# A third buffer for the multiplier pairs, a constant tile of ones in the prefix sums, and eight plain matmuls ahead of the third group of tiles

## The chip, the cores and the metric

The kernel runs as one program on one core of a Trainium2 chip. The metric is the device time of one execution in microseconds (us); several executions are timed and their median counts. One further execution is recorded by the hardware profiler, and all rows below come from that one. The engines are named as in the profile: PE multiplies matrices, DVE and ACT work on vectors, POOL fills constants and issues some transfers, SP issues most transfers. PEld is the loading of PE's weights, and a letter q behind a name (SPq) is the engine's queue of instructions that only issue or wait.

## The reference

Three layers follow one another, all in float32.

```python
# 1. linear attention with a complex, data-dependent decay; B, H, S, D = 4, 8, 768, 48
mag = np.sqrt(a_re * a_re + a_im * a_im)
scale = np.minimum(mag, 0.999) / (mag + 1e-06)
a_re_n, a_im_n = (a_re * scale, a_im * scale)
for t in range(S):
    new_re = ar * S_re - ai * S_im          # ar, ai: a_re_n, a_im_n at t
    new_im = ar * S_im + ai * S_re
    S_re, S_im = (new_re + k_t outer v_t, new_im)
    y[:, :, t] = einsum('bhd,bhde->bhe', q[:, :, t], S_re)
# 2. top-1 mixture of experts on the 3072 rows of y: 384 -> 1024 -> 384, 8 experts
out[mask] = gate_w[mask, None] * (np.maximum(xe @ w1[e], 0.0) @ w2[e])
# 3. a second layer on all rows
a = x @ w1
b = x @ w2
return ((a * b @ w3) @ w_out)
```

(`k_t outer v_t` stands for the einsum of the keys and values of one time step.)

## The kernel before, in words

The 768 time steps are cut into three groups (NG), and a group into eight pieces (NPC, 24 pieces in all). Two streams of work are interleaved by `drive` (L742).

The first stream, `elementwise` (L804), goes through the pieces on ACT and DVE. For a piece it loads the multipliers a_re and a_im (`load_a`, L786; one load brings the pair of pieces i and i + 1, 768 KB into one buffer of the tag "a"), squares them on ACT and sums the squares (`root`, L821, called three pieces ahead), makes the normed coefficients (`excess`, `norm`; the product at L843 is the last reader of a pair's buffer), forms the running products of the coefficients step by step on DVE (`prefix`, L852: one product at L862 and one sum at L864 for each time step), and scales queries and keys by them (`keys`, L881; the last product is L894). The sums of squares are made on PE for some pieces (L818) and on DVE for the others (L814). The queries and keys of a piece come by `load_qk` (L798, the load at L801, three buffers). The result of a piece is stored to the memory tensor qkd (L899 to L902). `self.stored` is the tile of the last result.

The second stream, `groups` (L1108), does the attention of a group on PE once the eight pieces of that group are made. `ends` (L949) transposes the group's last running product, copies it to the tile T and, ahead of the first and the second group, lets PE do the eight matmuls of `dense` (L961), whose result nobody reads. Then it loads the keys and values of two units (`loads`, L980; kk from qkd at L991, vz at L989), transposes them (L975), and goes through the eight units of the group. `chain` (L1040) carries the state from unit to unit on PE, ACT and DVE (L1060, L1061, L1067, L1074 to L1076); `scores` (L994), `outputs` (L1011) and `route` (L111) fill the time between. Output tiles are routed to experts and scattered to memory by POOL (L162).

When the last piece is done, the pools of the first stream are closed, and the weights w_out and w3 of the third layer are loaded into their memory (L293, tag "fdr") and split into two halves by `halves` (L315) on DVE and ACT. From about 408 us on PE multiplies them (L352 to L354), then the experts run (`moe`, L444), and last the third layer (`moe2`, L540). `route_end` (L231) makes the prefix sums over the experts with `scan` (L176); two other calls of `scan` are in `segments`, in a branch that these inputs do not take.

Tiles are named by tag, and a planner sets the order of each engine's instructions and the buffer of each tile when the program is built: it simulates the engines with times of its own and takes what is ready first. A tile that takes the memory of a closed pool waits for the readers of what lay there. On the chip the order of every engine and queue is then fixed, and each engine works strictly in this order.

Of the kernel before, what the change touches and what calls it, by code (L numbers as in the profile page):

```python
# [9 lines left out]
F32 = mybir.dt.float32  # L10
# [5 lines left out]
ALU = mybir.AluOpType  # L16
# [7 lines left out]
NE = 8  # L24
# [148 lines left out]
    return pr[:, :NE]  # L173


def scan(nc, sp, src, nm):  # L176

    one8 = sp.tile([128, NE], F32, tag="one8", name="one8" + nm)
    nc.vector.memset(one8, 1.0)
    inc = sp.tile([128, NE], F32, tag=nm + "i", name=nm + "i")  # L180
    nc.vector.tensor_tensor_scan(out=inc, data0=one8, data1=src, initial=0.0, op0=ALU.mult, op1=ALU.add)
    ex = sp.tile([128, NE], F32, tag=nm + "e", name=nm + "e")
    nc.vector.tensor_tensor(out=ex, in0=inc, in1=src, op=ALU.subtract)
    return inc, ex


def segments(tc, S, sp):

    nc = tc.nc
    n = sp.tile([128, NE], F32, tag="ntot", name="ntots")  # L190
    nc.vector.tensor_tensor(out=n, in0=totals(tc, S, "s"), in1=S.ebase, op=ALU.subtract)
    _, off = scan(nc, sp, n, "so")
    seg = sp.tile([128, NE], F32, tag="seg", name="seg")
    nc.vector.tensor_scalar(out=seg, in0=n, scalar1=0.0, scalar2=S.bad, op0=ALU.is_gt, op1=ALU.mult)
    for s in range(NP, NT, NP):
        nc.vector.scalar_tensor_tensor(out=seg, in0=n, scalar=float(s), in1=seg, op0=ALU.is_gt, op1=ALU.add)
    cin, cex = scan(nc, sp, seg, "sc")
    nc.vector.tensor_copy(S.nsegi, cin[:, NE - 1 : NE])
    si = sp.tile([128, MAXSEG], I32, tag="si", name="si")
    nc.gpsimd.iota(si, pattern=[[1, MAXSEG]], base=0, channel_multiplier=0)  # L200
    sf = sp.tile([128, MAXSEG, 1], F32, tag="sf", name="sf")
    nc.vector.tensor_copy(sf[:, :, 0], si)
    t78 = lambda nm: sp.tile([128, MAXSEG, NE], F32, tag=nm, name=nm)
    sfb = sf.to_broadcast([128, MAXSEG, NE])
    soh = t78("soh")
    nc.vector.tensor_tensor(out=soh, in0=sfb, in1=bc(cex, MAXSEG, 1), op=ALU.is_ge)
    s2 = t78("s2")
    nc.vector.tensor_tensor(out=s2, in0=sfb, in1=bc(cin, MAXSEG, 1), op=ALU.is_lt)
    nc.vector.tensor_tensor(out=soh, in0=soh, in1=s2, op=ALU.mult)
    st = t78("st")  # L210
    nc.vector.tensor_tensor(out=st, in0=sfb, in1=bc(cex, MAXSEG, 1), op=ALU.subtract)
    skip = sp.tile([128, 1], F32, tag="skip", name="skip")
    nc.vector.tensor_scalar(out=skip, in0=S.bad, scalar1=float(-NP), scalar2=float(NP), op0=ALU.mult, op1=ALU.add)
    nc.vector.tensor_scalar(out=st, in0=st, scalar1=float(NP), scalar2=skip, op0=ALU.mult, op1=ALU.add)
    nl = sp.tile([128, NE], F32, tag="nl", name="nl")
    nc.vector.tensor_scalar(out=nl, in0=n, scalar1=float(-NP), scalar2=0.0, op0=ALU.add, op1=ALU.max)
    nc.vector.tensor_tensor(out=st, in0=st, in1=bc(nl, MAXSEG, 1), op=ALU.min)
    tab = sp.tile([128, 3, MAXSEG], F32, tag="tabf", name="tabf")
    tmp = t78("tmp")
    for r, base in enumerate((S.ebase, off, S.eidx)):  # L220
        if r < 2:
            nc.vector.tensor_tensor(out=tmp, in0=st, in1=bc(base, MAXSEG, 1), op=ALU.add)
            nc.vector.tensor_tensor(out=tmp, in0=tmp, in1=soh, op=ALU.mult)
        else:
            nc.vector.tensor_tensor(out=tmp, in0=soh, in1=bc(base, MAXSEG, 1), op=ALU.mult)
        nc.vector.reduce_sum(out=tab[:, r], in_=tmp, axis=AX.X)
    nc.vector.tensor_copy(S.tab, tab)
# [3 lines left out]
def route_end(tc, S, sp):  # L231

    nc = tc.nc
    n = sp.tile([128, NE], F32, tag="ntot", name="ntote")
    nc.vector.tensor_tensor(out=n, in0=totals(tc, S, "e"), in1=S.ebase, op=ALU.subtract)
    _, off = scan(nc, sp, n, "off")
    nc.vector.tensor_copy(S.offi, off)
    most = sp.tile([128, 1], F32, tag="most", name="most")
    nc.vector.reduce_max(out=most, in_=n, axis=AX.X)
    nc.vector.scalar_tensor_tensor(out=S.rare, in0=most, scalar=float(NP), in1=S.bad, op0=ALU.is_gt, op1=ALU.max)  # L240
    dlt = sp.tile([128, NE], F32, tag="dlt", name="dlt")
    nc.vector.tensor_tensor(out=dlt, in0=off, in1=S.ebase, op=ALU.subtract)
    step = sp.tile([128, NE], F32, tag="step", name="step")
    nc.vector.tensor_copy(step, dlt)
    nc.vector.tensor_tensor(out=step[:, 1:], in0=dlt[:, 1:], in1=dlt[:, : NE - 1], op=ALU.subtract)
    sh = sp.tile([128, NTT, NE], F32, tag="sh", name="sh")
    nc.vector.tensor_tensor(out=sh, in0=S.pos.unsqueeze(2).to_broadcast([128, NTT, NE]), in1=bc(S.ebase, NTT, 1), op=ALU.is_ge)
    nc.vector.tensor_tensor(out=sh, in0=sh, in1=bc(step, NTT, 1), op=ALU.mult)
    pk = sp.tile([128, NTT], F32, tag="pk", name="pk")
    nc.vector.reduce_sum(out=pk, in_=sh, axis=AX.X)  # L250
    nc.vector.tensor_tensor(out=pk, in0=pk, in1=S.pos, op=ALU.add)
    nc.vector.tensor_copy(S.pki, pk)
    ex = sp.tile([128, NTT, NE], F32, tag="ex", name="ex")
    nc.vector.tensor_tensor(out=ex, in0=S.lg, in1=S.mx.to_broadcast([128, NTT, NE]), op=ALU.subtract)
    nc.scalar.activation(out=ex, in_=ex, func=AF.Exp)
    sm = S.cpool.tile([128, NTT], F32, tag="sm", name="sm", bufs=2)
    nc.vector.reduce_sum(out=sm, in_=ex, axis=AX.X)
    nc.vector.tensor_scalar(out=sm, in0=sm, scalar1=1e-9, scalar2=None, op0=ALU.add)
    nc.vector.reciprocal(sm, sm)
    S.sm = sm  # L260
# [364 lines left out]
D = 48  # L625
C = 64
NG = 3
TP = 8
NPC = C // TP
NPIECE = NG * NPC  # L630
# [11 lines left out]
WARM = 8  # L642
# [135 lines left out]
class Attn:  # L778
# [6 lines left out]

    def load_a(self, i):  # L786

        a = self.ep.tile([128, 2, 2, TP * D], F32, tag="a", name=f"a{i}", bufs=2)
        g, p = divmod(i, NPC)
        src = self.S.a[g].rearrange("r l (p e) -> p l r e", e=TP * D)  # L790
        if i:
            self.nc.sync.dma_start(a, src[p : p + 2].rearrange("n l r e -> l r n e"))
        else:
            for n in range(2):
                self.nc.sync.dma_start(a[:, :, n], src[n])
        return [a[:, :, n] for n in range(2)]
# [7 lines left out]
    def elementwise(self, aside, factors):  # L804

        nc, S, ep, e2 = self.nc, self.S, self.ep, self.e2
# [3 lines left out]
        a, sq, pu, y0, cf, P, s2, px, raw = ({} for _ in range(9))  # L810
# [106 lines left out]
        def chain(*gens):  # L917
            for x in gens:
                yield from x

        for i in (0, 2):
            a[i], a[i + 1] = self.load_a(i)
        raw[0] = self.load_qk(0)
        for i in range(AHEAD):
            root(i)
        yield from chain(excess(0), norm(0), excess(1))
        for i in range(NPIECE + 1):
            if i:
                power(i - 1)
                weigh(i - 1)  # L930
            if i % 2 and i + 3 < NPIECE:
                a[i + 3], a[i + 4] = self.load_a(i + 3)
            if i + AHEAD < NPIECE:
                root(i + AHEAD)
            if i + 1 < NPIECE:
                raw[i + 1] = self.load_qk(i + 1)
            ends = [j >= 0 and j % NPC == NPC - 1 for j in (i - 2, i - 1)]
            rest = [keys(i - 2)] if i > 1 and not ends[0] else []
            if i + 1 < NPIECE:
                rest.append(norm(i + 1))  # L940
            if ends[1]:
                rest.append(keys(i - 1))
            if i + 2 < NPIECE:
                rest.append(excess(i + 2))
            yield from mix(*([prefix(i)] if i < NPIECE else []), chain(*rest))
            if i == NPIECE - 1:
                factors()

    def ends(self, g):  # L949
        nc, S = self.nc, self.S  # L950
        pt = self.pp.tile([R2, 4, 128], F32, tag="tr", name=f"trT{g}", bufs=2)
        for r in range(2):
            nc.tensor.transpose(pt[:, r], self.last[g][:, r].rearrange("p r d -> p (r d)"), self.S.ident)
        self.T = self.st.tile([R2, 2, 2, 4, 2 * NH], F32, tag="T", name=f"T{g}")
        for r in range(2):
            nc.scalar.copy(self.T[:, r].rearrange("e q c (k i h) -> e (q c k) i h", k=2, i=2), pt[:, r].rearrange("e (x h i) -> e x i h", h=NH // 2, i=2))
        if g < NG - 1:
            self.dense(self.stored[:, :512], WARM)
        yield 480

    def dense(self, x, n):  # L961
# [450 lines left out]
```

## Time and profile before

| | |
|---|---|
| median of 3 timed runs | 1000.36 us (999.25 to 1002.5) |
| the profiled execution | 1003.89 us; its span from the first to the last instruction 1002.1 us |
| busy in the span | PE 898.0 us (90%), DVE 609.6 us (61%), ACT 488.5 us (49%), POOL 130.3 us (13%) |
| mean granted clock of PE | 0.946 of full speed |
| instructions | 17063 |

Times within the profile count from the start of the span. Busy time is the time in which an engine executes; a share of it over the whole span mixes stages with different limits, so the stages are read one by one below. An idle time stands in square brackets behind an instruction, with the instruction whose end released it.

### The profile page before, as it was taken

To read this page: it belongs to the slowest core of one execution; us is meant where nothing else is said; L and a number is where in the kernel's file an instruction comes from. 1 tells how busy PE (TensorE), PEld (TensorE's weight loads), DVE (VectorE), ACT (ScalarE), POOL (GpSimd) and SP (SyncE) were. 2 spreads that over 40 slices of the span, in tenths; PEclk is the share of its full clock that TensorE was granted. 3 is DMA by queue.
4 is the path that set the end of the run, shared out by engine and by line. 5 is a ranking of instruction groups with operands and counts; after the bars stand their busy time and mean duration, and the time that the engine had idled before them with its cause. 6 is when DMAs were issued, how large, how long until landed. Compare 5 with 4: busy or idle time off the path is not lost. (4 is left out here: it accounts for less than half of the span.)

```text
span 1002.1 us, 17063 instructions
## 1 busy us (share of the span) xinstructions
PE 898.0 (90%) x6402; PEld 764.9 (76%) x6402; DVE 609.6 (61%) x1374; ACT 488.5 (49%) x1089; POOL 130.3 (13%) x197
## 2 busy tenths in 40 slices
PE   3444899868898999999989999998999999999997
PEld 1222468655786788989979999997888888888886
DVE  6899889798798596576489995443232323232222
ACT  6454588774775687444456665443231312121211
POOL 5111000202002102100232201110000000000001
PEclk8666899998897799999999999999999999999999
DMA  5555976429643985553677655640000000000000
GB/s 189 179 179 182 291 251 201 145 95 306 191 144 127 333 265 159 162 175 107 199 205 183 187 133 137 126 85 2 1 9 24 9 24 9 24 5 28 9 24 31
DMA packets 90182, 128.74 MB, mean 128 GB/s; under 512 B 7232, under 2 KB 72688, under 8 KB 90096
## 3 DMA queue, kind: packets, MB, share of 16 engines
q1 hardware_dynamic: 76300, 82.61, 29.1%
q0 software_dynamic: 10688, 40.36, 11.4%
q10 hardware_dynamic: 3108, 4.65, 1.6%
q8 instruction: 51, 0.84, 0.4%
q14 instruction: 35, 0.29, 0.1%
HBM read 92.38 MB, written 35.22 MB: 127 GB/s over the span
## 5 line engine op out<-in xcount | busy, mean ns | idle before, releaser
L608 DVE TENSOR_TENSOR ab<-asb,pb 128x512 f32<-128x512 f32 x48 | 33.0, 687 | 188.2 <-PE pb L354 184.2
L347 ACT CAST h<-w 128x384 fp32r<-128x384 f32 x128 | 65.5, 514 | 96.5 <-PE ph L353 48.9
L348 DVE TENSOR_TENSOR l<-w,h 128x384 fp32r<-128x384 f32 x128 | 70.5, 554 | 63.7 <-ACT h L347 59.0
L603 ACT COPY asb<-pa 128x512 f32<-128x512 f32 x48 | 28.1, 586 | 121.6 <-PE pa L354 117.0
L818 PE MATMUL x<-s,ident 128*128 128x384 f32 x64 | 35.6, 692 | 49.1 <-ACT s L870 49.0
L347 ACT CAST gh<-ab 128x512 fp32r<-128x512 f32 x48 | 29.7, 620 | 94.7 <-DVE ab L608 90.2
L353 PE MATMUL py<-hl,h 128*128 128x432 f32 x192 | 70.1, 365 | 3.9 <-DVE hl L409 3.9
L352 PE MATMUL py<-hh,h 128*128 128x432 f32 x192 | 69.3, 361 | 2.5 <-ACT hh L408 2.5
L352 PE MATMUL ph<-xh,h 128*128 128x432 f32 x192 | 69.6, 363 | 0.0
L354 PE MATMUL ph<-xh,l 128*128 128x432 f32 x192 | 69.4, 361 | 0.0
L353 PE MATMUL ph<-xl,h 128*128 128x432 f32 x192 | 69.3, 361 | 0.0
L354 PE MATMUL py<-hh,l 128*128 128x432 f32 x192 | 69.1, 360 | 0.0
L862 DVE TENSOR_TENSOR pr<-cf,P 128x192 f32<-128x192 f32 x189 | 66.6, 353 | 3.2
L353 PE MATMUL po<-ol,gh 128*128 128x384 f32 x192 | 64.9, 338 | 0.0
L352 PE MATMUL po<-oh,gh 128*128 128x384 f32 x192 | 64.8, 337 | 0.0
L818 PEld LDWEIGHTS x<-s,ident 128*128 128x128 f32 x64 | 15.0, 257 | 64.6 <-ACT s L870 55.6
L354 PE MATMUL po<-oh,gl 128*128 128x384 f32 x192 | 64.1, 338 | 0.0
L572 POOL DMA_INDIRECT out<-ob,mdp x24 | 23.8, 993 | 305.4 <-DVE ob L571 163.7
L975 PE MATMUL tr<-ident,kk 128*96 128x128 f32 x384 | 57.3, 282 | 5.9 <-DMA kk<-qkd 3.5
L976 ACT COPY qkT<-tr 96x512 f32<-96x512 f32 x96 | 53.4, 590 | 15.6 <-PE tr L975 15.1
L352 PE MATMUL pa<-yh,ah 128*128 128x512 f32 x144 | 57.1, 396 | 3.0 <-ACT yh L347 3.0
L353 PE MATMUL pb<-yl,bh 128*128 128x512 f32 x144 | 57.0, 396 | 0.0
(219 smaller groups left out, 2397.7 us busy)
## 6 DMA issues: line engine op xcount, KB each, us to landing
w<-in_w SPq DMA_DIRECT2D x128, 192.0 KB
kk<-qkd SPq DMA_DIRECT2D x24, 768.0 KB
qkd<-qk POOLq DMA_DIRECT2D x21, 768.0 KB, 6.7
qkr<-in_qk SPq DMA_DIRECT2D x24, 384.0 KB
a<-in_a SPq DMA_DIRECT2D x11, 768.0 KB
fdr<-in_w SPq DMA_DIRECT2D x16, 512.0 KB
fdr<-in_v POOLq DMA_DIRECT2D x12, 512.0 KB, 6.3
xs<-zr POOLq DMA_DIRECT2D x8, 648.0 KB, 7.9
```

What stands on the lines that cost most here:

```text
L347: nc.scalar.copy(H, src)
L348: nc.vector.tensor_tensor(out=L, in0=src, in1=H.bitcast(F32), op=ALU.subtract)
L352: nc.tensor.matmul(out, lh, rh, start=first, stop=False)
L353: nc.tensor.matmul(out, lh, rl, start=False, stop=False)
L354: return nc.tensor.matmul(out, ll, rh, start=False, stop=last)
L572: nc.gpsimd.indirect_dma_start(out=S.outv[j], out_offset=bass.IndirectOffsetOnAxis(ap=S.mdp[:, j, 0:1], axis=0), in_=ob, in_offset=None, b ...
L603: nc.scalar.copy(asb, pa)
L608: nc.vector.tensor_tensor(out=ab, in0=asb, in1=pb, op=ALU.mult)
L818: nc.tensor.matmul(p, S.ident, s[r], start=r == 0, stop=r == 1)
L862: v.tensor_tensor(out=pr, in0=twice(cf[i][:, t]), in1=bc(pv, 2, 1), op=ALU.mult)
L975: nc.tensor.transpose(pt[:, h], qk[:, h0 + h, w], self.S.ident)
L976: nc.scalar.copy(qkT[:, w, h0 : h0 + 4], pt)
```

## The change

Three edits. The tag "a" gets three buffers in place of two, one more pair is loaded at the start, and the loads in the loop bring the pair i + 5 in place of i + 3. `scan` reads its ones from a constant tile in place of a tile that it fills itself. The condition in `ends` goes, so that the eight matmuls of `dense` are issued ahead of the third group too.

```diff
-def scan(nc, sp, src, nm):
-
-    one8 = sp.tile([128, NE], F32, tag="one8", name="one8" + nm)
-    nc.vector.memset(one8, 1.0)
+def scan(S, nc, sp, src, nm):
+
     inc = sp.tile([128, NE], F32, tag=nm + "i", name=nm + "i")
-    nc.vector.tensor_tensor_scan(out=inc, data0=one8, data1=src, initial=0.0, op0=ALU.mult, op1=ALU.add)
+    nc.vector.tensor_tensor_scan(out=inc, data0=S.ones[:, :NE], data1=src, initial=0.0, op0=ALU.mult, op1=ALU.add)
...
-        a = self.ep.tile([128, 2, 2, TP * D], F32, tag="a", name=f"a{i}", bufs=2)
+        a = self.ep.tile([128, 2, 2, TP * D], F32, tag="a", name=f"a{i}", bufs=3)
...
         raw[0] = self.load_qk(0)
+        a[4], a[5] = self.load_a(4)
         for i in range(AHEAD):
             root(i)
...
-            if i % 2 and i + 3 < NPIECE:
-                a[i + 3], a[i + 4] = self.load_a(i + 3)
+            if i % 2 and i + 5 < NPIECE:
+                a[i + 5], a[i + 6] = self.load_a(i + 5)
...
-        if g < NG - 1:
-            self.dense(self.stored[:, :512], WARM)
+        self.dense(self.stored[:, :512], WARM)
         yield 480
```

The three callers of `scan` pass S as well. `dense` itself is unchanged:

```python
    def dense(self, x, n):
        w = self.adds.tile([128, 512], F32, tag="ad", name="dense", bufs=2)
        for _ in range(n):
            self.nc.tensor.matmul(w[:, : x.shape[-1]], self.S.ident, x, start=True, stop=True)
```

## Rows read from the trace of the kernel before

**Rows 1.** The windows view: start:end, length, busy us by engine, PEclk, DMA share, GB/s.

```profile
0.00:108.20 108.20, 48.73 (x82) 23.65 (x82) 89.56 (x223) 58.02 (x121) 24.85 (x86) 0.72 0.58 192
108.20:226.40 118.20, 104.06 (x1154) 78.09 (x1154) 102.84 (x258) 89.73 (x235) 9.39 (x13) 0.96 0.59 187
226.40:322.80 96.40, 85.46 (x1105) 68.41 (x1106) 83.01 (x209) 63.16 (x164) 12.75 (x16) 0.89 0.60 195
322.80:332.40 9.60, 8.43 (x69) 6.67 (x67) 4.15 (x19) 2.89 (x8) 0.57 (x1) 0.68 0.81 217
332.40:413.00 80.60, 78.06 (x1129) 67.14 (x1130) 57.64 (x150) 57.27 (x142) 14.06 (x10) 0.97 0.73 232
413.00:692.00 279.00, 270.51 (x1430) 257.17 (x1429) 189.22 (x393) 143.25 (x296) 44.81 (x47) 0.99 0.56 148
```

**Rows 2.** The waits view: waiter, releaser, us in total, times, longest.

```profile
ACT sq L823 <- DMA a<-in_a: 22.3, 10, 4.4
...
SPq L792 <- DVE cf L843: 20.9, 8, 7.2
```

**Rows 3.** DVE in order of time: start, length, line, [idle before it and releaser].

```profile
28.50 0.56 DVE L887 TENSOR_TENSOR s<-x,s 128x384 f32<-128x384 f32 x1 [1.17 <-PE u L818]
...
44.64 0.56 DVE L831 TENSOR_TENSOR sq<-u,sq 128x384 f32<-128x384 f32 x1 [2.66 <-ACT sq L828]
...
66.76 0.56 DVE L831 TENSOR_TENSOR sq<-u,sq 128x384 f32<-128x384 f32 x1 [0.72 <-ACT sq L828]
...
87.72 0.56 DVE L831 TENSOR_TENSOR sq<-u,sq 128x384 f32<-128x384 f32 x1 [0.70 <-ACT sq L828]
...
135.24 0.56 DVE L839 SCALAR_TENSOR_TENSOR sq<-sq,y 128x384 f32<-128x384 f32 x1 [1.68 <-ACT y L837]
...
177.45 0.56 DVE L814 TENSOR_TENSOR sq<-sq 128x384 f32<-128x384 f32 x1 [0.30 <-ACT sq L823]
...
217.83 0.56 DVE L814 TENSOR_TENSOR sq<-sq 128x384 f32<-128x384 f32 x1 [1.25 <-ACT sq L823]
...
255.13 0.56 DVE L814 TENSOR_TENSOR sq<-sq 128x384 f32<-128x384 f32 x1 [4.66 <-ACT sq L823]
```

**Rows 4.** Order of time on SP, ACT and PE around the last pair's load.

```profile
243.72 0.37 SPq L792 DMA_DIRECT2D a<-in_a  x1
...
254.16 0.84 ACT L823 ACTIVATE sq<-a 128x768 f32<-128x768 f32 x1 [4.45 <-DMA a<-in_a]
...
257.25 0.45 PE L1022 MATMUL y<-z,qkT 96*64 96x48 f32 x2 [3.81 <-ACT xo L1026]
```

**Rows 5.** DVE in order of time: idle stretches without a pair's load behind them.

```profile
62.18 0.56 DVE L887 TENSOR_TENSOR s<-x,s 128x384 f32<-128x384 f32 x1 [0.32 <-ACT s L879]
...
197.69 0.69 DVE L1007 TENSOR_TENSOR at<-sc,mask 128x512 f32<-128x512 f32 x1 [4.76 <-PE x L818]
...
249.75 0.56 DVE L814 TENSOR_TENSOR s<-s 128x384 f32<-128x384 f32 x1 [0.97 <-ACT s L870]
```

**Rows 6.** The seam ahead of the third group: DVE, PE, and two windows.

```profile
320.99 1.76 DVE L894 TENSOR_TENSOR qk<-P,qkr 128x1536 f32<-128x1536 f32 x1
...
332.40 1.94 PE L975 MATMUL tr<-ident,kk 128*96 128x128 f32 x8 [0.90 <-DMA kk<-qkd]
...
324.35:332.40 8.05, 6.88 (x34) 5.17 (x32) 2.73 (x17) 2.88 (x7) 0.00 (x0) 0.68 0.90 246
332.40:339.07 6.67, 5.71 (x32) 5.36 (x32) 0.99 (x3) 3.29 (x12) 3.98 (x4) 0.62 1.08 363
```

**Rows 7.** PE in order of time: the plain matmuls at the first two seams.

```profile
108.24 8.83 PE L965 MATMUL dense<-qk,ident 128*128 128x512 f32 x16 [2.34 <-DVE qk L894]
...
226.48 9.68 PE L965 MATMUL dense<-qk,ident 128*128 128x512 f32 x16 [2.18 <-DVE qk L894]
```

**Rows 8.** SP's loads of w_out at the third seam, and the memset's line.

```profile
330.14 4.04 SPq L293 DMA_DIRECT2D fdr<-in_w_out  x5
...
L179 DVE MEMSET one8off<- x1: 65/65/65, 328.2 to 328.2; 128x8 f32 x1
```

More of the change, by code (lines that the diff above doesn't have):

```diff
@@ L191, in segments @@
     nc.vector.tensor_tensor(out=n, in0=totals(tc, S, "s"), in1=S.ebase, op=ALU.subtract)
-    _, off = scan(nc, sp, n, "so")
+    _, off = scan(S, nc, sp, n, "so")
     seg = sp.tile([128, NE], F32, tag="seg", name="seg")
@@ L196, in segments @@
         nc.vector.scalar_tensor_tensor(out=seg, in0=n, scalar=float(s), in1=seg, op0=ALU.is_gt, op1=ALU.add)
-    cin, cex = scan(nc, sp, seg, "sc")
+    cin, cex = scan(S, nc, sp, seg, "sc")
     nc.vector.tensor_copy(S.nsegi, cin[:, NE - 1 : NE])
@@ L235, in route_end @@
     nc.vector.tensor_tensor(out=n, in0=totals(tc, S, "e"), in1=S.ebase, op=ALU.subtract)
-    _, off = scan(nc, sp, n, "off")
+    _, off = scan(S, nc, sp, n, "off")
     nc.vector.tensor_copy(S.offi, off)
```

## The prediction

> **What bounds the kernel now.** I read the stages first, then the waits of ACT and SP, then DVE's order of time with the idle stretch ahead of each instruction, and last PE's order at the seams between the groups. The stage table [rows 1] shows three stretches of the scan (0 to 108.2, 108.2 to 226.4, 226.4 to 322.8 us): each ends when the last piece of a group has been multiplied out and stored, and only then can PE fetch that group's keys. DVE is busy 89.56 of 108.20, 102.84 of 118.20 and 83.01 of 96.40 us there, more than any other engine in the first and about level with PE in the other two. After the seam of 9.6 us PE does one more group (78.06 of 80.60 us) and then has work without a break (270.51 of 279.00 us). So a microsecond taken from the first 323 us moves all that follows; one taken from DVE after it moves nothing.
>
> The loads of the multiplier pairs show in the waits: ACT stood 22.3 us in ten waits for them, and SP stood 20.9 us in eight waits for the product that frees a pair's buffer [rows 2]. The loads are late because they are issued late. ACT's wait counts only where DVE runs dry behind it, and [rows 3] is the list of these: eight places, each with its idle time and its releaser (the square itself, or what is made from it on PE or stands behind it in ACT's queue). The place at 255.13 us is the clearest [rows 4]: SP issues the last pair at 243.72, ACT can square it at 254.16 after 4.45 us of standing, DVE has then stood 4.66 us, and PE 3.81 us, because its outputs wait for a copy that stands behind the square in ACT's queue.
>
> **The change part by part.** *Third buffer, loads two pieces earlier.* Each pair's load moves up by two pieces; a stage has eight pieces, so two are 24 to 30 us by [rows 1]. The longest load took 10.44 us from issue to use (243.72 to 254.16, [rows 4]), so every pair from the third on should have landed before it is asked for, and SP need no longer stand for a buffer either, as the one it writes was freed two pieces earlier. On SP the load passes two loads of queries and keys and whatever the attention has put between; it waits for nothing itself, so nothing new stands behind it. The first pair's wait, at the start, stays; it is at most the 4.4 us of the longest in [rows 2].
>
> What DVE gets back, by stage, from [rows 3]:
> - First stage: 1.17 + 2.66 + 0.72 + 0.70 = 5.25 us. Behind each, the next late operand is ACT's exponential; where it comes last, it costs 0.32 us [rows 5]. I take four of these off: 5.25 - 4 x 0.32 = 4.0 us. No attention runs here, so nothing else can take the place.
> - Second stage: 1.68 + 0.30 + 1.25 = 3.23 us. ACT is busy 89.73 of 118.20 us and PE 104.06 [rows 1], both serving the first group's attention in the same queues. I take half, 1.6 us.
> - Third stage: 4.66 us, less 0.97 us, which the operand next to it was late [rows 5]: 3.7 us.
>
> Sum 9.3 us; the bounds are 0 (each wait replaced by another one) and 13.1 us (5.25 + 3.23 + 4.66).
>
> A rule speaks against early loads: the Trainium skill, "DMA: Bandwidth & Descriptors", section "Issuing engines are not separate DMA queues", says that transfers run on the same 16 engines and interleave, whoever issued them. By that rule a pair that landed beside a group's first keys would push them by its 768 KB at the 363 GB/s of [rows 6], 2.2 us, and the time would be 994.3; the trace agrees in that the load of 243.72 took 10.44 us beside them, but that load is just the one that moves out of this place.
>
> *Eight plain matmuls at the third group.* They are 16 instructions on PE, and at the first two seams these took 8.83 and 9.68 us [rows 7]; both times PE had first stood 2.34 and 2.18 us for the product that they read. At the third seam that product ends at 322.75, and the keys arrive at 332.40, where PE stands 0.90 us for them [rows 6]. Before, PE is busy 6.88 of the 8.05 us from 324.35 to 332.40 at a mean clock of 0.68, and 5.71 of the 6.67 us after it at 0.62 [rows 6]: that is between the levels of 1.2 and 2.4 GHz, and the same work at full clock is 6.88 x 0.68 = 4.7 and 5.71 x 0.62 = 3.5 us (estimates from these rows); the lower clock costs 6.88 x 0.32 + 5.71 x 0.38 = 4.4 us there. Three placements bound the price:
> - the other work of the seam is done before 322.75: the matmuls end at 322.75 + 9.68 = 332.43, as the keys arrive, and what follows takes 3.5 instead of 6.67 us: a gain of 3.1 us;
> - they go in at 324.35, behind the last outputs of the second group (where the windows of [rows 6] are cut): 324.35 + 8.83 + 4.7 = 337.9, and 3.5 behind it 341.4, against 339.07: a loss of 2.3 us;
> - they are queued ahead of these outputs and PE stands for the product as at the earlier seams: 2.3 us more, a loss of 4.6 us.
>
> I take a loss of 1.0 us: nearest to the second, since the row at 324.35 has no free 9 us, but less, as PE gains more from the pair of 254 us than DVE does (3.81 us of standing and the clock behind it) and so comes to the seam earlier. The routing steps that they push back (from 324.35 on) feed only scatters to memory. One wait is new: the matmuls read the last product after its pool has been closed, and the loads of w_out into that memory now wait for them. SP issues these at 330.14 [rows 8], so it could stand up to about 3 us (332.43 less 330.14, plus some), with the third unit's keys behind; the work for w_out on DVE that is fed by it has 80.60 - 57.64 = 23 us of room in its stage [rows 1]. I cost that at nothing; without this room it would be those 3 us.
>
> The Trainium skill, "TensorE: Matmul & The Clock Gate", section "Terms", prices time at the lower clock at that time x (1 - 1/2). By that rule the seam's 10.2 us at half clock (an estimate from the two means of the clock) are worth 5.1 us instead of my 4.4, and the whole sum would come out 0.7 us lower, 991.4; the rows say less, because PE stood idle for part of it.
>
> *Ones from the constant tile.* One memset of 65 ns leaves DVE at 328.2, where DVE is half idle [rows 8]; the two other scans are in the branch not taken. Nothing.
>
> **Sum.** 1002.1 - 9.3 + 1.0 = 993.8 us of span. The profiled execution took 1003.89 us, 1.8 above its span, and the median of the three timed runs is 1000.36, 3.5 below the profiled one. So 993.8 + 1.8 - 3.5 = 992.1, said as 992.0.
>
> **Rivals.**
> *All of it, and a warm PE.* No wait takes the place of another (13.1 us) and the matmuls fit the seam (3.1 us): 1000.4 - 16.2 = 984. For it: the first and third stages name the load alone. Against it: the seam's 8.05 us are already 6.88 us full.
> *Only the first stage pays.* From 108 us on PE, ACT and DVE hang on each other; DVE's saved time turns into waits for PE, and the matmuls cost 2.3 us: 1000.4 - 4.0 + 2.3 = 998.7. For it: PE is busy 104.06 of 118.20 and 85.46 of 96.40 us there, the third stage at a mean clock of 0.89 [rows 1]. Against it: PE too was standing at 254.
> *The reordered queues make new convoys: slower.* The order on each engine is written by a planner from its own times, and the buffer count is one of its inputs. Squares and roots that may start earlier are put ahead of the attention's copies on ACT and of its matmuls on PE, and DVE stands behind. The price of one such convoy is in the trace: 4.76 us at 197.69, DVE waiting for a mask product behind sums on PE [rows 5]. From the second new one on (9.5 us) the gain of 8.3 is gone; with three, 992.1 + 14.3 = 1006.4. For it: one such convoy exists with no load near it. Against it: it is one in 215 us.
> *The buffer does nothing* would need the loads to be bound by transfer; with 10.44 us the longest, that is left out.
>
> **How the numbers follow.** Forecast 0.52, all of it 0.13, first stage only 0.19, convoys 0.16. The timed runs of before lie within 0.3% of one another, so faster and slower mean beyond 0.3% (997.4 and 1003.4 us). Faster: nearly all of the first case, the second, and a little of the third, 0.67. Same: most of the third and the edges of the first and fourth, 0.18. Slower: 0.15. The range from 984 to 1002 leaves out the upper end of the second case and most of the fourth; the forecast's own is 987 to 997.
>
> **What would show it.** Right: the sum of ACT's waits for the pairs falls from 22.3 us to the first one's, at most 4.4, SP's waits for the product that frees a pair are gone, the eight idle places of DVE are 0.3 us or less, and the last product of the third group ends near 313 instead of 322.75. The matmuls stand on PE right behind that product, the clock is at 1.0 when the keys arrive, and from there to the end of the trace the length is about 1 us more than the 669.7 us of before (1002.1 - 332.4, with the arrival taken from the same product). Wrong: the waits for the pairs gone but the third product not earlier than 318 (another wait took their place), the keys of the third group later behind their product than 9.7 us (the transfers collide), or PE standing in front of the matmuls with outputs of the second group queued behind.

## Result and the profile after

The changed kernel takes 1008.05 us (median of six runs, 1006.52 to 1011.51) against 1000.22 (six runs): ratio 1.0085, 95% interval 1.0064 to 1.0106, so slower by some 8 us where 8 less were forecast. Its profiled execution took 1008.58 us, span 1006.9. Line numbers in the other kernels are one or two lower than before (L892 of after is L894 of before).

ACT's waits for the pairs went as forecast; SP's for a free buffer did not. The waits views of ACT and SP after, to be read against [rows 2]:

```profile
ACT sq L821 <- DMA a<-in_a: 3.2, 2, 2.9
...
SPq L790 <- DVE cf L841: 13.2, 7, 3.7
```

With the third buffer SP still stood 13.2 us (20.9 before) for the product that frees a pair's buffer. The pairs were issued early enough all the same: ACT's two waits are all that is left.

The windows view after; columns as in [rows 1], cut where the last product of each group ends, where the third group's first keys arrive, and at 413 us:

```profile
0.00:102.40 102.40, 50.20 (x82) 23.88 (x82) 89.25 (x223) 58.99 (x124) 25.08 (x86) 0.73 0.64 211
102.40:216.50 114.10, 104.96 (x1154) 79.37 (x1154) 107.96 (x275) 89.53 (x233) 9.79 (x13) 0.94 0.61 194
216.50:304.80 88.30, 79.72 (x1059) 64.36 (x1059) 77.24 (x193) 60.06 (x154) 13.52 (x16) 0.93 0.63 205
304.80:314.50 9.70, 3.64 (x81) 3.45 (x81) 1.42 (x2) 3.32 (x13) 0.57 (x1) 0.82 0.83 224
314.50:413.00 98.50, 92.97 (x1143) 74.37 (x1144) 61.02 (x160) 57.97 (x141) 10.81 (x10) 0.90 0.56 179
413.00:692.00 279.00, 273.09 (x1454) 260.14 (x1453) 189.78 (x396) 142.76 (x297) 44.69 (x47) 0.99 0.57 151
```

The three stages are 5.8, 4.1 and 8.1 us shorter than in [rows 1], and the third product ends 18 us earlier. The third group then gives all of it back and more. Its yardstick below is the stretch from the end of the last product (DVE, L894 before, L892 after) to the end of the last output copy (ACT). The windows view of that stretch, before and after, same columns:

```profile
322.75:408.67 85.92, 82.21 (x1168) 69.56 (x1166) 61.24 (x166) 58.94 (x146) 14.63 (x11) 0.93 0.74 230
```

```profile
304.80:413.02 108.22, 96.64 (x1223) 77.84 (x1224) 62.44 (x162) 61.31 (x154) 11.38 (x11) 0.89 0.59 183
```

85.9 us became 108.2. PE has 14.4 us more busy time in it, 7.13 of which are the eight matmuls; 7.9 us more are idle (11.6 against 3.7), and the mean clock is lower (0.89 against 0.93). From the last output to the end of the span both kernels take the same: 1002.1 - 408.67 = 593.4 and 1006.9 - 413.02 = 593.9 us. So what is lost is lost in the third group. PE's order of time at its seam, after:

```profile
308.26 0.32 PE L1021 MATMUL y<-vz,at 128*64 128x48 f32 x4
314.49 1.06 PE L973 MATMUL tr<-ident,kk 128*96 128x128 f32 x4 [5.91 <-DMA kk<-qkd]
...
324.08 0.33 PE L1001 MATMUL sc<-qkT 96*64 96x64 f32 x2
324.34 7.13 PE L963 MATMUL dense<-qk,ident 128*128 128x512 f32 x16
331.41 0.34 PE L1001 MATMUL sc<-qkT 96*64 96x64 f32 x4
```

The keys arrive 314.49 - 304.80 = 9.69 us behind the product (9.65 before), so nothing collides with them. The matmuls take 7.13 us (8.83 and 9.68 at the earlier seams [rows 7]), but they do not stand behind the product, as forecast: they start 19.5 us after its end, among the score matmuls of the first unit. SP's waits view shows what hangs on them, the loads of w_out; SP issues these 26.7 us behind the product (at 331.54) in place of 7.4 [rows 8]:

```profile
SPq L291 <- PE dense L963: 6.9, 1, 6.9
```

### The profile page after: what moved, and what is told of

It reads as the page before. It is cut to its first block, busy times and chain, and to the rows that moved or that the text cites. A ratio compares the mean times of both kernels' runs of the same rounds, so it can differ in the third digit from the quotient of the medians.

```text
span 1006.9 us, 17092 instructions
## 1 busy us (share of the span) xinstructions
PE 910.6 (90%) x6418; PEld 771.8 (77%) x6418; DVE 609.9 (61%) x1373; ACT 488.3 (48%) x1089; POOL 128.2 (13%) x197
## 5 line engine op out<-in xcount | busy, mean ns | idle before, releaser
L973 PE MATMUL tr<-ident,kk 128*96 128x128 f32 x384 | 61.5, 293 | 12.3 <-DMA kk<-qkd 11.0
L860 DVE TENSOR_TENSOR pr<-cf,P 128x192 f32<-128x192 f32 x189 | 66.6, 353 | 3.3
L973 PEld LDWEIGHTS tr<-ident,kk 128*96 128x96 f32 x384 | 43.4, 135 | 22.1 <-issue 9.9
```

What stands on the lines that cost most here:

```text
L860: v.tensor_tensor(out=pr, in0=twice(cf[i][:, t]), in1=bc(pv, 2, 1), op=ALU.mult)
L973: nc.tensor.transpose(pt[:, h], qk[:, h0 + h, w], self.S.ident)
```

## Experiments

Eighteen kernels were run. "Product" is the end of the third group's last product, "group" the time from there to the end of the last output copy, "units" the time from the first to the eighth output copy of that group, "w3 wait" what VectorE stood for w3's loads in it; these are from one profile each (that of e4 took 7.4 us more than e4's median, that of e2 4.4 more). The ratio is to the kernel before, on the same chip.

| run | ratio, 95% interval | product | group | units | w3 wait |
|---|---|---|---|---|---|
| before | 1 | 322.8 | 85.9 | 62.0 | 0.6 |
| after | 1.0085, 1.0064-1.0106 | 304.8 | 108.2 | 73.5 | 3.6 |
| e1_no_third_dense | 1.0049, 1.0030-1.0069 | 305.1 | 101.0 | 74.6 | 6.7 |
| e2_dense_alone | 1.0213, 1.0192-1.0235 | 317.8 | 103.5 | 73.0 | 6.0 |
| e3_dense_of_ones | 1.0044, 1.0021-1.0067 | 305.3 | 101.1 | 67.9 | 4.5 |
| e4_dense_in_tr | 1.0102, 1.0069-1.0136 | 306.6 | 111.4 | 80.0 | 6.2 |
| f1_no_early_split | 1.0050, 1.0015-1.0085 | 310.4 | 99.9 | 72.5 | 2.9 |
| f4_before_no_early_split | 1.0101, 1.0035-1.0168 | 318.6 | 86.2 | 61.9 | 0 |
| g1_prefetch_fill2400 | 1.0001, 0.9976-1.0027 | 308.1 | 97.7 | 71.6 | 3.3 |
| g2_before_fill2800 | 1.0030, 1.0003-1.0057 | 322.5 | 92.5 | 64.5 | 0.6 |
| i1_first_stage_only | 0.9970, 0.9950-0.9989 | 315.6 | 86.8 | 61.7 | 0.7 |
| i2_first_two_stages | 1.0085, 1.0055-1.0114 | 310.0 | 102.2 | 72.3 | 4.2 |
| h2_split_held_back | 1.0383, 1.0333-1.0434 | 306.7 | 95.4 | 64.1 | none split |
| h3_before_split_held_back | 1.0442, 1.0412-1.0472 | 318.5 | 86.3 | 62.9 | none split |
| k1_w3_held_back | 1.0180, 1.0132-1.0228 | 312.6 | 91.1 | 66.6 | none split |
| k2_before_w3_held_back | 1.0246, 1.0198-1.0295 | 320.0 | 84.1 | 60.1 | none split |
| k4_seven_small_buffers | 1.0075, 1.0046-1.0103 | 313.8 | 98.7 | 73.7 | 1.4 |
| j1_pairs_4_and_22 | 1.0014, 0.9977-1.0051 | 315.6 | 92.9 | 65.0 | 1.7 |
| m1_prefetch_old_order | 0.9918, 0.9894-0.9942 | 308.2 | 87.1 | 61.6 | 0.4 |
| m2_first_stage_new_order | 1.0090, 1.0060-1.0120 | 311.1 | 100.1 | 75.8 | 6.8 |

The product's end differs from profile to profile among kernels that load the pairs alike: from 318.5 to 322.8 us in before, f4, h3 and k2 (mean 320.0), from 304.8 to 313.8 in the ten kernels with the prefetch in all stages (mean 308.2). The group and the units are therefore counted from within each profile.

**The parts of the change.** e1 leaves the third batch out of the changed kernel:

```diff
-        self.dense(self.stored[:, :512], WARM)
+        if g < NG - 1:
+            self.dense(self.stored[:, :512], WARM)
```

> The changed kernel without the eight matmuls at the third seam: third buffer, earlier pair loads and constant ones stay. Theory A (the third batch of dense matmuls spoils the third group): the last output of the second group comes near 308.6 us as in the changed kernel, and the third group takes the 83.7 us that it took before, so the time is near 985 us (982 to 990). Theory B (the third group is longer because the prefetch changes the order of its work, and the matmuls cost only the 7.1 us that they run): near 1001 us (998 to 1004), with the third group at some 97 us.

e2 is the kernel before with that condition taken out and nothing else.

> The kernel before with the eight matmuls at the third seam and nothing else. Theory A: the matmuls hold TensorE and the w_out loads here too, so it is slower than before, 1004 to 1012 us; the third group is longer than 83.7 us. Theory B: they cost at most their own run of 7.1 us, part of it in the gap 324 to 332 us in which TensorE was idle: 1000 to 1007 us.

e3 lets the third batch read ones, e4 lets it write a buffer of the transposes' tag:

```diff
+            w = self.adds.tile([128, 512], F32, tag="ad", name="dense", bufs=2).rearrange("p (a b) -> p a b", a=4)
+            for _ in range(WARM):
+                nc.tensor.matmul(w, S.ident, bc(S.ones, 4, 1), start=True, stop=True)
```

```diff
+            w = self.pp.tile([128, 512], F32, tag="tr", name="dense", bufs=2)
```

> The changed kernel with the third batch reading a constant tile of ones in place of the stored product: same count, width and PSUM buffer, but no hold on the memory of the group's product, so the six w_out loads need not wait for it. Theory A1 (the wait of the w_out loads is what costs): the loads issue near 309 us, VectorE splits w_out some 20 us earlier, and the time falls to 985 to 995 us. Theory A2 (the place of the matmuls in TensorE's stream, inside the first unit, is what costs): the loads come early but the time stays at 1003 to 1009 us. Theory B: 1003 to 1009 us as well.

> The changed kernel with the third batch writing a PSUM buffer of the transposes' tag in place of the one that it shares with the router's tiles. It then stands earlier in TensorE's stream. Theory A (it came late because the router held its buffer): it runs in the idle stretch 308 to 316 us before the keys, the w_out loads issue some 15 us earlier, and the time is 984 to 995 us. Theory B: 998 to 1009 us, since the third group's order is as long without it.

Theory A falls with e1: without the matmuls the group still takes 101.0 us, and the kernel is slower than before. The median, 1002.7 us, lies in theory B's range. e2 is a miss for both: the matmuls alone cost 20 us, more than their 7.1 (and the gap that theory B counted on was not idle: PE was busy 6.88 of its 8.05 us [rows 6]). They too lengthen the units, from 62.0 to 73.0 us, where none of them stand. e4 does put the matmuls early (306.62 us, 0.05 behind the product) and gains nothing. e3, in which w_out's loads need not wait for the matmuls, is level with e1; as the orders of e3, e1 and the changed kernel all differ, that does not show what the matmuls or the wait cost in the latter.

**Is it VectorE standing for weights, or the order?** In the changed kernel and in e1 to e4 VectorE stands for w3's loads (last column), and in e1 PE's longest idle place in the middle of the group lies behind that. VectorE and PE in e1, order of time:

```profile
350.47 0.16 DVE L143 TENSOR_REDUCE kx<-key 128x2 f32<-128x16 f32 x1
351.96 0.43 DVE L337 TENSOR_SCALAR fdl<-fdr 128x512 uint16<-128x512 uint16 x1 [1.33 <-DMA fdr<-in_w]
...
353.11 0.17 DVE L145 TENSOR_TENSOR oh<-key,kx 128x16 f32<-128x16 f32 x1
```

```profile
353.33 0.39 PE L149 MATMUL rk<-oh,upper 128*128 128x16 f32 x2 [2.44 <-DVE oh L145]
```

The split (L337) waits for its data, the router's step (L145), ready since 350.63, stands behind it, and PE stands 2.44 us for that, 1.33 of them VectorE's wait. f1 and f4 take the early calls of the splitting out of e1 and of before; g1 and g2 change FILL, which sets how much filling work goes between two steps of the chain:

```diff
-                        if side.fuse.ready < min(BEFORE, side.fuse.blocks + W3B):
-                            next(singles, None)
+                        pass
```

```diff
-FILL = 2600
+FILL = 2400
```

> The prefetching kernel without the third batch, and without the splitting of w_out and w3 during the third group: all of it is made after the last output. The whole time is some tens of us longer by that and says nothing; what is read is the third group, from the last output copy of the second group to the last one of the third: 83.7 us in the kernel before, 97 us with the prefetch. Theory C (VectorE stands in its fixed order in front of a split whose weights have not landed, the attention's steps stand behind it, TensorE runs dry and its clock falls): the group shrinks to 85 us or less, TensorE's idle places of over 2 us in its middle go. Theory D (the planner wrote a poorer order of the attention itself): it stays above 92 us.

> The kernel before without the splitting of w_out and w3 during the third group; all of it is made after the last output, so the whole time is some tens of us longer and says nothing. The third group is read: 83.7 us before. Theory C: at most 3 us shorter, since VectorE stood only 0.6 us for w3 there. Theory D: within 5 us either way, as the planner writes the order anew.

> The prefetching kernel without the third batch and with FILL 2400 in place of 2600 (how much filling work goes between two steps of the chain): the same instructions, in the first two groups nearly the same order, in the third another one. Theory D (the third group's length is an accident of the order): it moves by 4 us or more from 97 us, and the time with it from 1002.7 us, in either direction. Theory C: VectorE's waits for w3 stay, and the time stays within 3 us of 1002.7 us.

> The kernel before with FILL 2800 in place of 2600, nothing else: another order of the same instructions in the third group, 60 and 121 TensorE rows moved in the two groups ahead. Theory D: the kernel before holds a good order of its third group, another one costs it 4 us or more: 1002 to 1012 us. Theory C: within 3 us of before, as the loads and the splits stand as they stood.

f1 and f4 missed their aim: in both, 16 splits stood in the third group as before, since the planner takes what is ready. f1 counts as another order of the same work. f4 is the order of before once more: of PE's 1095 rows from the third group's first keys to its last output (matmuls of `dense` and of the third layer's weights left out) all stand in the trace in the same sequence. g1 was 4.8 us faster than e1 by the ratios and g2 3.0 us slower than before; the first is what theory D forecast, the second lies at the border of theory C (within 3 us), though its group is 6.6 us longer. The long group stays long in three orders (101.0, 99.9, 97.7 us), and the short one becomes longer in another order (92.5 against 85.9), which still leaves a third theory, E: something that does not move with the product ends the group near 405 us. i1 and i2 give the extra buffer to some pairs only (i1 to the pair of piece 4, i2 also to that of piece 10); h2 and h3 bind all splitting behind the last routing step, in e1 and in before:

```diff
-        a = self.ep.tile([128, 2, 2, TP * D], F32, tag="a", name=f"a{i}", bufs=3)
+        a = self.ep.tile([128, 2, 2, TP * D], F32, tag="ax" if i in (4,) else "a", name=f"a{i}", bufs=1 if i in (4,) else 2)
```

```diff
-        for n, _ in enumerate(self._bound(halves(S, nc, raws, wp, first), lambda: [S.end])):
+        for n, _ in enumerate(self._bound(halves(S, nc, raws, wp, first), lambda: S.gate)):
```

> The extra buffer for one pair alone (pieces 4 and 5), so that the pairs of the first stage come early and from piece 10 on the pairs wait as in the kernel before; constant ones, no third batch. TensorE's order is that of the kernel before, row for row; VectorE's and ScalarE's differ in 12 and 6 rows at the start. Theory D (what the prefetch gains is lost to the newly written order of the third group): with the old order the gain of the first stage stays, product and last output come 5 us earlier, 0.5% faster than before (ratio 0.993 to 0.997). Theory E (something that does not move with the product ends the third group near 405 us): the product comes 5 us earlier, the last output does not, ratio 1.000.

> The extra buffer for two pairs (pieces 4 and 5, 10 and 11): the first two stages have their pairs early, the third waits as before; constant ones, no third batch. TensorE's order differs from before by 76, 835 and 70 rows in the three groups, so the third group keeps nearly the old order. Theory D: the third product near 313 us and a third group (product to last output) of 86 to 90 us as before: ratio 0.990 to 0.997. Theory E: last output at 405 us again, ratio 1.000. Theory C: as D if VectorE's waits for w3 stay under 1 us, else 4 to 6 us more.

> The prefetching kernel without the third batch, with all splitting of w_out and w3 bound behind the last routing step of the third group, so that none of it stands on VectorE between the attention's steps. The whole time is some tens of us longer by that and says nothing. Read is the third group, product to last output: 86 us in the kernel before, 98 to 101 us with the prefetch. Theory C (VectorE stands for w3 in front of the attention): 84 to 90 us, no falling clock at 40 to 55 us behind the product. Theory D (order of the attention): 92 us or more. (Taking out only the early calls of the splitting had left it in the third group, as the planner takes what is ready.)

> The kernel before with the same binding: all splitting behind the last routing step of the third group; the whole time says nothing. Product to last output: theory C 83 to 86 us, hardly less than the 86 us of before, since VectorE hardly stood for w3 there; theory D: anything from 80 to 95 us, as the order is written anew.

Theory E falls with i1: PE's order is that of before, the product comes earlier, the group is 86.8 us as before, the last output ends at 402.4, and the kernel is faster. i2 was expected short, with the third group's TensorE order nearly that of before, and is long (102.2). The traces show that this premise was wrong: of before's 1095 PE rows of the third group i2 keeps 857 in sequence (i1 and f4 all 1095, e1 804). So i2 is one more new order, and no case against theory D; its second group's tail also ran 10.2 us past the product. h2's group, 95.4 us, is on theory D's side (92 or more), though its units are short: without any splitting they take 64.1 us in h2 and 62.9 in h3. That looks like a share of theory C, but h2 and h3 also have nearly one order (1055 of 1095 PE rows in sequence), so the pair cannot tell the two theories apart. What is left of the difference between their groups, 8 of 9 us, lies at the seam, where the first output comes 31.3 us behind the product in h2 and 23.4 in h3.

Next, w3 alone was held back (k1 in e1, k2 in before: its units in a list of their own, bound to `S.gate`); k4 keeps w3 in and takes the wait away, with smaller loads in more buffers; j1 gives the extra buffer to the pairs of pieces 4 and 22, `i in (4, 22)`.

```diff
-        raws = ahead(doubles(self.w2p, nc.sync, 5), srcs, 4)
+        raws = ahead(doubles(self.w2p, nc.sync, 7, 384), srcs, 6)
```

> The prefetching kernel without the third batch, with the splitting of w3 alone bound behind the last routing step of the third group (w_out is split inside it as before); the whole time is longer by what w3 then costs and says nothing. Read is the time from the first to the eighth output of the third group: 72 to 75 us with the prefetch, 62 us before, 64 us with all splitting held back. Theory C (VectorE stands for w3's loads in front of the attention's steps): 62 to 66 us. Theory D (the order of the attention itself): 70 us or more.

> The kernel before with the same binding of w3; the whole time says nothing. First to eighth output of the third group: theory C 60 to 63 us, as VectorE hardly stood for w3 there (0.6 us); theory D: anything from 58 to 72 us, as the order is written anew.

> The prefetching kernel without the third batch; w3 comes in loads of 384 columns in place of 512, in seven buffers of 3 KB a partition in place of five of 4 KB, six loads ahead in place of four. Theory C: VectorE's waits for w3 in the third group fall from 6.7 us to under 2, first to eighth output 62 to 67 us, time 6 to 9 us below the prefetch alone: ratio to before 0.990 to 0.998. Theory D: 70 us or more, ratio 1.000 to 1.010; the twelve smaller splits in place of eight cost VectorE a few us either way.

> The extra buffer for two pairs, pieces 4 and 5 and the last pair (22 and 23), whose load was late by 4.66 us on VectorE in the kernel before. TensorE's order is that of before in the first two stages; 130 rows of the second group and 309 of the third stand otherwise. Theory C: product near 311 us (5 us of the first stage, 4 of the last pair); ratio 0.990 to 0.995 if VectorE's waits for w3 stay under 1 us in the third group, near 1.000 if they are 3 us or more. Theory D: with the third group's order new the last seven units take 70 us or more whatever VectorE's waits for w3 are, ratio 1.000 or more.

k1 (66.6 us) lies between C and D, but k4 speaks against it: VectorE's wait fell to 1.4 us, the idle place of 2.44 us in the middle is gone, and the units still took 73.7. j1 fits neither number: 65.0 us with another order. So taking the wait away did not make the units short.

**The orders exchanged.** At the end of the program each engine's instructions of the third group are tied one behind the other, in the order read from the other kernel; m1 is e1 with i1's order (PE's of before, row for row), m2 is i1 with e1's order.

```diff
+    for names in ORDERS:
+        seq = [found[f"I-{n}"] for n in names.split() if f"I-{n}" in found]
+        for p, i in zip(seq, seq[1:]):
+            tc.add_manual_dep(i, p.name, mybir.DependencyInfo(mybir.DependencyClass.NoSync, mybir.DependencyReason.DATA), reason="in_order")
```

> The prefetching kernel without the third batch (extra buffer in all stages), with the instructions of the third group bound on every engine to the order that they have in the kernel with the extra buffer in the first stage alone, which is the order of the kernel before. The first two groups keep the prefetching kernel's order. Theory D (the order of the third group loses the gain): product at 305 to 310 us as with the prefetch, product to last output 86 to 91 us in place of 98 to 101, ratio to before 0.982 to 0.992. Theory E (the group is longer for any order once it starts early): product to last output 95 us or more, ratio 0.997 to 1.006.

> The reverse: the extra buffer in the first stage alone, and the third group bound on every engine to the order that the planner wrote for the prefetching kernel. Theory D: product at 314 to 318 us, product to last output 96 to 101 us in place of 87, ratio to before 1.005 to 1.015. Theory E: product to last output 86 to 90 us, ratio 0.995 to 1.000.

Both came out as theory D says, but for m2's product, which came at 311.1 us where 314 to 318 was expected. In the traces m1 has all of i1's PE rows of the third group in their sequence, and m2 all of e1's. Windows from product to last output, columns as above: e1, then m1, then i1, then m2.

```profile
305.07:406.06 100.99, 90.38 (x1206) 76.76 (x1207) 61.33 (x162) 61.02 (x154) 14.38 (x11) 0.87 0.61 196
```

```profile
308.25:395.40 87.15, 78.80 (x1127) 66.68 (x1126) 60.93 (x165) 58.69 (x144) 10.79 (x11) 0.94 0.71 227
```

```profile
315.57:402.41 86.84, 81.54 (x1168) 68.83 (x1166) 61.03 (x165) 59.14 (x146) 10.77 (x11) 0.94 0.72 228
```

```profile
311.09:411.20 100.11, 88.88 (x1209) 73.83 (x1209) 61.15 (x162) 61.56 (x154) 16.28 (x11) 0.90 0.63 198
```

The length follows the order (101.0 and 100.1 with the new one, 87.1 and 86.8 with the old), not the product's time. In the four profiles with the old order (before, f4, i1, m1) the units take 61.6 to 62.0 us. The windows from the first to the eighth output copy, e1 and then m1, show where the 13.0 us between them lie:

```profile
331.46:406.06 74.60, 66.63 (x954) 55.69 (x954) 51.02 (x130) 47.39 (x116) 13.81 (x10) 0.93 0.52 167
```

```profile
333.83:395.39 61.56, 59.91 (x930) 50.98 (x929) 48.53 (x126) 46.56 (x116) 6.23 (x6) 1.00 0.60 191
```

PE stands 8.0 us in e1 and 1.7 in m1, and its mean clock is 0.93 against 1.00, which is worth up to 74.60 x 0.07 = 5.2 us (an estimate from these rows). Even VectorE's wait for w3 comes with the order: it is 0.4 us in m1, with e1's buffers and loads, and 6.8 in m2. Waits views of VectorE, m1 and then m2, over the same stretches:

```profile
DVE fdl L337 <- DMA fdr<-in_w: 0.4, 1, 0.4
```

```profile
DVE fdl L337 <- DMA fdr<-in_w: 6.8, 6, 2.3
```

What is poor in e1's order shows best at the last unit. PE in e1 and in m1, order of time, the rows between left out; L1066 makes the last unit's state product, and L1059 can start only when ScalarE (L1073) and VectorE (L1074, L1075) have worked on it:

```profile
389.83 0.69 PE L1002 MATMUL sc<-qkT 96*64 96x64 f32 x16
...
393.55 1.60 PE L1066 MATMUL W<-vz,kk 128*96 128x96 f32 x16
394.98 0.49 PE L123 MATMUL rt<-ident,xo 128*128 128x128 f32 x3
398.91 2.06 PE L1059 MATMUL W<-cb,perm 96*96 96x384 f32 x4 [3.43 <-DVE W L1075]
401.85 0.46 PE L1021 MATMUL y<-z,qkT 96*64 96x48 f32 x4 [0.89 <-ACT z L1060]
...
405.09 0.45 PE L1022 MATMUL y<-vz,at 128*64 128x48 f32 x4
```

```profile
385.20 1.60 PE L1066 MATMUL W<-vz,kk 128*96 128x96 f32 x16
...
390.36 1.53 PE L1059 MATMUL W<-cb,perm 96*96 96x384 f32 x4
391.72 0.49 PE L123 MATMUL rt<-ident,xo 128*128 128x128 f32 x3
392.77 0.33 PE L1021 MATMUL y<-z,qkT 96*64 96x48 f32 x4 [0.55 <-ACT z L1060]
...
394.56 0.32 PE L1022 MATMUL y<-vz,at 128*64 128x48 f32 x4
```

In the old order the state product stands ahead of the seventh unit's outputs, which then cover the steps of ScalarE and VectorE. In the new one it stands behind them: PE has nothing left and stands 3.43 us. Behind that the last outputs take 405.54 - 401.85 = 3.69 us in place of 394.88 - 392.77 = 2.11. The same place is in m2 (398.91 there is 403.43, again 3.43 us), and so is the one in the middle. PE in m2:

```profile
357.39 0.40 PE L149 MATMUL rk<-oh,upper 128*128 128x16 f32 x2 [2.36 <-DVE oh L145]
...
403.43 2.81 PE L1059 MATMUL W<-cb,perm 96*96 96x384 f32 x4 [3.43 <-DVE W L1075]
```

The Trainium skill, "PSUM — Partial Sum Buffer", section "Engine vs sequencer instructions", says that VectorE's queue is strictly first in, first out. The traces agree: the step at 353.11 us in e1 had its operand from 350.63 on and stood behind the split that waited.

m1 is the fastest of all: 992.88 us (ten runs, 990.69 to 994.53) against 1001.26 for before on the same chip.

The exchange was made with e1, not with the changed kernel, whose order is a third one. That has such places too, elsewhere. PE in the changed kernel, and the window around this place:

```profile
359.57 0.34 PE L1021 MATMUL y<-vz,at 128*64 128x48 f32 x1 [2.19 <-DVE at L1005]
```

```profile
355.50:369.20 13.70, 11.52 (x102) 8.82 (x102) 11.24 (x29) 6.83 (x19) 0.00 (x0) 0.50 0.73 226
```

VectorE's step (L1005) stands behind splits that waited for w3, and PE's clock is 0.50 for 13.7 us.

## Why the prediction was wrong

**The step that failed** is the first one: "a microsecond taken from the first 323 us moves all that follows", with "from there to the end of the trace the length is about 1 us more than the 669.7 us". Measured from the keys on it was 1006.9 - 314.5 = 692.4 us, 22.7 more. The prediction took the third group's length as given. It is given only for a given order, and the planner wrote a new one, because the buffer count is one of its inputs. That order (e1's) costs 101.0 - 87.1 = 13.9 us (e1 against m1, the same buffers) or 100.1 - 86.8 = 13.3 (m2 against i1), a little more than the prefetch gains.

- *Prefetch, 9.3 us.* Right in kind: ACT's waits for the pairs fell from 22.3 to 3.2 us. A little too small: in the one profile of the changed kernel the stages gave 5.8, 4.1 and 8.1 us where 4.0, 1.6 and 3.7 were taken, but part of these 18 us is the spread between executions; the means over the four and the ten profiles above give 5.0, 1.9 and 4.9 us, 11.8 in sum. The 4 x 0.32 us taken off the first stage were not due: VectorE's waits for ACT's exponential (0.22 to 0.32 us) stand in both kernels, and no new ones came. Two side readings were wrong without harm: SP did go on standing for buffers (13.2 us), and the longest load took 11.25 us from issue to use (120.48 to 131.73 in before), not 10.44.
- *A term that the sum lacked.* Stages that are shorter than the attention of the group ahead leave a tail of that attention in the next group: the second group's last output copy ended 2.2 us behind the third product before, 4.3 in the changed kernel and 7.0 in e1. Its price was not measured apart.
- *Matmuls, 1.0 us.* Mis-sized, and for the wrong place. None of the three placements had them 19.5 us behind the product, and the clock was not at 1.0 when the keys arrived (0.51 from 311.0 to 321.4 us after). With the prefetch they add 108.2 - 101.0 = 7.2 us to the group, their whole length, and the ratios differ by 0.0036, 3.6 us; the order differs as well, so neither is their price alone. On the kernel before they cost 20 us (e2). Its third group has a new order too (911 of before's 1095 PE rows in sequence), but that this is the reason is argued, not shown: no exchange was made there.
- *New wait of the w_out loads, costed at nothing.* It is there, at 6.9 us (up to 3 were forecast). Whether it costs was not separated from the order.
- *Ones from the constant tile, nothing.* Nothing speaks against it: i1, which holds it, keeps PE's order of before, and its group takes 86.8 us (85.9 before).
- *Rivals.* "Convoys" (1006.4, chance 0.16) is the one that came: slower, through queues that the planner reordered, VectorE and PE standing behind each other. It was placed on ACT's squares and in the first three stages; the convoys lie in the third group, behind splits and state products. A single one was priced at 4.76 us; the two places shown in e1 are 2.44 us and 3.43 us, the latter with 1.58 us of lower clock behind it. That three of them, 1006.4, come near the 1008.05 measured is luck, as the matmuls have a share in it that this rival did not count.
- *Keys later by a collision*, the skill's rule in the prediction: 9.69 against 9.65 us, no sign of it.

With the old order held, the prefetch alone (m1) gives 8.2 us (ratio 0.9918, interval 5.8 to 10.6), where the sum had 9.3 for it. That is near, though in part by terms that offset each other: the stage terms were a little small, and in m1's profile the group and what follows it were 1.2 and 0.9 us longer than in before.

What stays open: why nearly every order that the planner wrote for a group whose product comes early is poor by 10 us or more (e1, f1, g1, i2, k4), while j1's and g2's new orders cost 6 to 7; what the matmuls cost in the changed kernel and in e2 apart from the order. The planner's own times were not looked at.

## What to carry to other kernels

Where a planner writes the order, a change of a buffer count is a change of every queue behind it: compare the orders of the two programs first, and price the stages whose rows moved apart from those that kept them. To tell a change's own worth from its new order, tie the old order to the new program on every engine; here that turned 0.5% slower into 0.8% faster. And where a chain passes through other engines, its step belongs ahead of the independent work that can cover them, not behind: at the last unit that was the difference between no standing and 3.43 us.

## What the runs showed of the hardware

A short standing of PE cost twice here: in e1 the 3.43 us ahead of 398.91 are followed by the lower level of the clock (1.2 in place of 2.4 GHz). The windows view of e1, columns as above:

```profile
400.00:405.00 5.00, 4.11 (x61) 3.15 (x60) 0.00 (x0) 0.80 (x1) 0.00 (x0) 0.50 0.00 0
```

The granted clock is 0.50, and the last outputs take 1.75 times as long as in m1 (3.69 against 2.11 us). The Trainium skill, "TensorE: Matmul & The Clock Gate", section "Terms", prices the lower level at half the time spent in it, 1.85 of these 3.69 us; the rows show 3.69 - 2.11 = 1.58, so the price is a little under that here.
